# Idle matmuls, partly in fp32, around value units 1 and 2 of a decode attention block

## The chip, the cores and the metric

The kernel runs on one core of one Trainium2 chip. The metric is device microseconds (us) of one execution, the median of several. A profiled execution also gives a span, from its first to its last instruction; in the runs here the time is 1.8 to 2.4 us more than the span, and that difference varies, so where a few tenths matter this text compares spans. Before the prediction there were three timed runs of the kernel, 669.61 to 669.99 us, and one profiled run, 672.52 us (span 670.3).

## The reference, cut to what matters

```python
# B=8 sequences, one new token each; 32 query heads, 8 key/value heads, 8192 cached positions, Dh=128
h = layernorm(x) * (1 + ca) + sa                  # adaLN: sa .. gb come from silu(c) @ w_mod
q = (h @ wq) ...
p = softmax(q @ k_cache^T * Dh**-0.5)             # k_cache, v_cache: (8, 8, 8192, 128) bf16
x = x + ga * ((p @ v_cache) @ wo)
h = layernorm(x) * (1 + cb) + sb
x = x + gb * (relu(h @ w1 + b1)**2 @ w2 + b2)     # 512 -> 1792 -> 512
```

The two caches are 268 MB of the 283.65 MB that the kernel reads. All else is small.

## The kernel before

Per batch there are four key units and four value units of 4 MB (two heads each), loaded into a ring of four slots in the order k0..k3, v0..v3. TensorE transposes the keys and makes the scores; after the softmax it multiplies each value unit. A slot is loaded again once its reader is done. After the last batch's last value unit (which comes in four pieces) the MLP weights W1 and W2 are loaded into a freed slot, W2 in four pieces, so they are the last bytes to arrive.

`pe_stream` is a helper for matmuls whose result nobody reads: they only keep TensorE busy.

```python
def pe_stream(n, at):                       # n matmuls IDENT x (IDENT four times): 128x128 by 128x512, bf16
    rhs = IDENT[:, :].unsqueeze(1).to_broadcast([128, 4, 128])
    ts = [op("tensor", lambda e: e.matmul(
        bank(at).rearrange("p (a r) -> p a r", a=4), IDENT[:, :], rhs)) for _ in range(n)]
    return ts[0]
...
# softmax of a batch
t = op("vector", ... Dm ...)
pe_stream(5, 4)
t = op("tensor", lambda e: e.matmul(T_ps, R4[:], Dm[:]), [t, stg_free[3]])
... negm ...
pe_stream(5, 4)
... exps, transposes of P ...
# the value units of a batch, p = 0..3
for p in range(NP):
    ...
    for m in range(32):                     # value matmuls, wait for the load
        t = op("tensor", ... Obank[32*cg:32*(cg+1), :] ..., [loaded[n], k_rinv] + pmd[m // 8])
    t = op("vector", lambda e: e.tensor_copy(osb, Obank), [t])
    for i in range(4):                      # matmuls with SEL, wait for the copy
        t = op("tensor", ... oT_ps, osb[...], SEL[:, i, :] ..., [k_osb, k_all])
        if i == 0:
            released[n % NSLOT] = t         # the slot's next load may start
            ...
    if p == NP - 3:                         # value unit 1
        pe_stream(5, 4)
    ... norm_last = op("vector", ... oTn ...)
    if lastb and p == NP - 2:               # only in the last batch, after unit 2:
        k_proj = project(permute(...))      # 24 projection matmuls for heads of units 0..2
... last batch only: unit 3 in pieces (16 matmuls, then 8 fp32 ones for the projection, then 12, then a rest),
    layer norm, first layer (56 matmuls), second layer (56 matmuls, each waits for its W2 piece), output
```

Of the kernel before, what the change touches and what calls it, by code (L numbers as in the profile page):

```python
# [33 lines left out]
class Prog:  # L34
# [19 lines left out]
    def op(self, eng, fn, deps=()):  # L54
        o = Op(eng, fn, deps, None, self.at)
        o.tok = Tok(o, self.at)
        self.ops[eng].append(o)
        return o.tok
# [110 lines left out]
def bass_adaLN_cond__gqa_block_cached__dense_activation_squared_relu__decode_kernel(  # L169
    nc, A_x, A_k_cache, A_v_cache, A_wq, A_wo, B_x, B_w1, B_b1, B_w2, B_b2, c, w_mod, out):  # L170
    B, _, D = A_x.shape
    _, HKV, SK, DH = A_k_cache.shape
# [6 lines left out]
    NP = HKV // 2  # L179
# [7 lines left out]
    with ExitStack() as es:  # L187
# [26 lines left out]
        ONES = sb("ONES", [128, 128], FP32)  # L214
# [51 lines left out]
        bank = lambda i: PS[:, i, :]  # L266
# [4 lines left out]
        op, dma = Pg.op, Pg.dma  # L271
# [189 lines left out]
        def pe_stream(n, at):  # L461
            rhs = IDENT[:, :].unsqueeze(1).to_broadcast([128, 4, 128])
            ts = [op("tensor", lambda e: e.matmul(  # L463
                bank(at).rearrange("p (a r) -> p a r", a=4), IDENT[:, :], rhs)) for _ in range(n)]
            return ts[0]

        def key_tiles(n, k, half):

            src = tiles(n % NSLOT)
            toks = []  # L470
            for j in range(4):
                for i in range(8):
                    t = op("tensor", lambda e, j=j, i=i: e.matmul(  # L473
                        STG[j][:, i, :], src[:, 32 * k + 8 * j + i, :], IDENT[:, :], is_transpose=True),
                        [loaded[n], stg_free[j]])
                dst = KTb[:, half, 8 * j:8 * (j + 1), :]
                if (4 * k + j) % 8 in (1, 4, 7):
                    stg_free[j] = op("scalar", lambda e, j=j, dst=dst: e.activation(dst, STG[j], ACT.Copy), [t])  # L478
                else:
                    stg_free[j] = op("vector", lambda e, j=j, dst=dst: e.tensor_copy(dst, STG[j]), [t])  # L480
                toks.append(stg_free[j])
            return t, toks
# [40 lines left out]
        for b in range(B):  # L523
# [5 lines left out]
            for p in range(NP):  # L529
                n = 2 * NP * b + p  # L530
                for k in range(4):
                    t, toks = key_tiles(n, k, qn % 2)
                    if pend is not None:
                        maxes.append(scores(b, *pend))
                    if k == 3:
                        released[n % NSLOT] = score_first[0]
                        load(n + NSLOT)
                    pend = (p, k, qn % 2, toks)
                    qn += 1
# [3 lines left out]

            t = op("vector", lambda e: e.tensor_reduce(m1[:], m4[:], AX.X, ALU.max), maxes)
            t = op("vector", lambda e: e.tensor_scalar(Dm[:], Qmask[:], m1[:, 0:1], None, ALU.mult), [t, k_all])
            pe_stream(5, 4)
            T_ps = bank(7)[:, 0:4]
            t = op("tensor", lambda e: e.matmul(T_ps, R4[:], Dm[:]), [t, stg_free[3]])
            t = op("vector", lambda e: e.tensor_reduce(mq[:], T_ps, AX.X, ALU.max), [t])
            k_neg = op("vector", lambda e: e.tensor_scalar(negm[:], mq[:], -inv_sqrt, None, ALU.mult), [t])  # L550
            pe_stream(5, 4)
            exps = []
            for k in range(4):
                exps.append(op("scalar", lambda e, k=k: e.activation(  # L554
# [43 lines left out]
            for p in range(NP):  # L598
                if p == NP - 1:
                    Pg.at = "post" if lastb else (b, "b")  # L600
                n = 2 * NP * b + NP + p
# [3 lines left out]
                if not lastu:  # L605
                    for m in range(32):
# [4 lines left out]
                            tile_position=(0, 32 * cg)),  # L611
                            [loaded[n], k_rinv] + pmd[m // 8])
                    osb = O_sb[:, p % 2, :]
                    t = op("vector", lambda e, osb=osb, Obank=Obank: e.tensor_copy(osb, Obank), [t])  # L614
                    oT_ps = Obank[:, 0:8]
                    k_osb = t
# [6 lines left out]
                            if n + NSLOT < len(units):  # L623
                                load(n + NSLOT)
                    if p == NP - 3:
                        pe_stream(5, 4)
                    s_bank_free[p] = norm_last = op("vector", lambda e, p=p, b=b, oT_ps=oT_ps: e.tensor_tensor(  # L627
                        oTn_p[:, :, p, :, Pg.index(b)].rearrange("p h r o -> p h (r o)"), oT_ps.rearrange("p (h r) -> p h r", h=2), rinv_p[:, :, p, :], ALU.mult),
                        [t])
# [157 lines left out]
```

## Time and profile before

| | before |
|---|---|
| timed runs | 669.61, 669.77, 669.99 us |
| profiled run | 672.52 us, span 670.3 us, mean granted clock 0.894 |
| read from HBM | 283.66 MB |

Three lines of the page's slices (40 equal slices of 16.8 us; digits are tenths; PEclk is the granted TensorE clock):

```profile
PEclk9997996799969998799978998599977999699985
DMA  9999999999999999999999999999999999999994
GB/s 374 436 409 432 434 430 428 430 432 436 432 428 430 432 436 432 428 430 434 434 434 428 428 434 434 434 430 426 434 434 434 430 428 432 434 434 430 428 413 196
```

The DMA engines are busy throughout at 426 to 436 GB/s, except at the start and in the last two slices. The body of the kernel is bound by the transfers.

The timeline of TensorE (start us, duration us, line, operation, number of instructions, in brackets the idle time before and what ended it), first around the value units of batch 6, then the end, in the last batch:

```profile
563.67 1.24 PE L463 MATMUL PS<-IDENT 128*128 128x512 bf16 x5
566.41 1.91 PE L608 MATMUL PS<-ring,Pm 128*32 128x512 bf16 x32 [1.50 <-DMA ring<-in_A_v_cache_dram]
...
576.12 3.48 PE L608 MATMUL PS<-ring,Pm 128*32 128x512 bf16 x32 [6.75 <-DMA ring<-in_A_v_cache_dram]
...
585.84 5.51 PE L473 MATMUL PS<-IDENT,ring 128*128 128x128 bf16 x64 [5.17 <-DMA ring<-in_A_k_cache_dram]
...
641.76 1.24 PE L463 MATMUL PS<-IDENT 128*128 128x512 bf16 x5
644.12 3.58 PE L608 MATMUL PS<-ring,Pm 128*32 128x512 bf16 x32 [1.12 <-DMA ring<-in_A_v_cache_dram]
...
649.97 1.76 PE L517 MATMUL PS<-wo_sb,KTb 128*32 128x512 bf16 x24 [0.51 <-DVE KTb L512]
...
651.86 1.90 PE L662 MATMUL PS<-ring,Pm 128*32 128x512 bf16 x16
...
654.23 1.88 PE L673 MATMUL PS<-SELP,KTb 128*128 128x8 f32 x8
656.03 1.47 PE L662 MATMUL PS<-ring,Pm 128*32 128x512 bf16 x12
...
665.68 1.65 PE L737 MATMUL PS<-KTb,ring 128*128 128x8 bf16 x56 [0.97 <-DVE KTb L733]
```

Batches 0 to 6 have long waits for the next load behind units 1 and 2 and before the next key unit: a slower or faster TensorE changes nothing there. The last batch's unit 2 (at 644.12) takes 3.58 us for work that took 1.91 us in batch 6. After it TensorE hardly waits for a load again; the second layer (at 665.68) waited for VectorE, not for its weights.

The windows of the end (each line: window, its length, busy time of PE, PEld, DVE, ACT, POOL with the number of instructions, then granted clock, DMA share, GB/s):

```profile
640.80:644.20 3.40, 1.48 (x17) 0.58 (x17) 0.88 (x2) 0.00 (x0) 0.00 (x0) 1.00 0.91 390
644.20:647.60 3.40, 3.40 (x32) 1.03 (x32) 0.00 (x0) 0.00 (x0) 0.00 (x0) 0.50 0.99 419
647.60:651.00 3.40, 1.71 (x44) 0.92 (x44) 1.24 (x3) 0.00 (x0) 0.00 (x0) 1.00 0.98 402
651.00:654.40 3.40, 3.40 (x47) 1.33 (x36) 0.69 (x1) 0.00 (x0) 0.00 (x0) 0.50 1.04 411
654.40:668.00 13.60, 10.17 (x214) 7.93 (x214) 3.78 (x17) 0.27 (x1) 0.00 (x0) 0.50 0.55 217
```

In this run the changes of the clock lie on a grid: from the fall at 572.52 to the one at 644.20 there are 21 steps of 3.413 us. On this grid each window's clock answers to how full the one before it was: after 1.48 busy us of 3.40 the clock is halved, after a full window it is restored, after 1.71 us it is halved again. The window from 651.0 is full by its bars and the clock is not restored; it holds many matmuls of 8 columns, so the bars seem not to measure exactly what the clock follows. Below, work at half clock is called cold and work at full clock warm; the phase of a run is where its grid of clock windows lies.

### The profile page before, as it was taken

The page shows a single profiled execution, that of the slowest core. Times are in us where ns is not written, and L with a number is a line of the kernel's source. Part 1 is how long each engine was busy: PE and PEld are TensorE (multiplying, and loading weights), DVE is VectorE, ACT ScalarE, POOL GpSimd, SP SyncE. Part 2 cuts the span into 40 slices and gives each one's busy share as a digit, 9 for nine tenths or more (in the row PEclk, how much of TensorE's full clock was granted, in tenths as well). Part 3 has the DMA queues.
Part 4 walks back from the last instruction along what each step waited for, and adds up shares of the span by engine and source line. Part 5 has one row for each costly group of instructions (what it writes and reads, how often), then busy time and mean ns, then how long its engine had stood idle before and what let it go on. Part 6 is the DMA issues. An engine that isn't in the chain of part 4 may idle for free.

```text
span 670.3 us, 15469 instructions
## 1 busy us (share of the span) xinstructions
PE 498.0 (74%) x7056; PEld 340.4 (51%) x7056; DVE 302.5 (45%) x571; ACT 258.7 (39%) x289; POOL 18.4 (3%) x76
## 2 busy tenths in 40 slices
PE   3594963898549974699729985599746996299876
PEld 2384731775237741576308752377415763187425
DVE  1262731566216751467215661167414663066622
ACT  2152640466106650265405660166503662056600
POOL 7300000000000000000000000000000000000000
PEclk9997996799969998799978998599977999699985
DMA  9999999999999999999999999999999999999994
GB/s 374 436 409 432 434 430 428 430 432 436 432 428 430 432 436 432 428 430 434 434 434 428 428 434 434 434 430 426 434 434 434 430 428 432 434 434 430 428 413 196
DMA packets 12176, 283.85 MB, mean 423 GB/s; under 512 B 1250, under 2 KB 1283, under 8 KB 3588
## 3 DMA queue, kind: packets, MB, share of 16 engines
q1 hardware_dynamic: 12116, 283.65, 98.7%
q8 instruction: 9, 0.15, 0.1%
q10 hardware_dynamic: 48, 0.02, 0.0%
q14 instruction: 3, 0.02, 0.0%
HBM read 283.66 MB, written 0.01 MB: 423 GB/s over the span
## 4 chain that ended last, share of the span: by engine, by line
PE 51%; DMA 38%; ACT 6%; DVE 4%; issue 1%; SPq 0%; DVEq 0%
PE PS L473 35%; DMA ring<-in_A_k_cache_dram 32%; PE PS L490 9%; ACT P_sb L554 5%; DMA ring<-in_A_v_cache_dram 4%; PE PS L608 3%; DMA ring<-in_A_wq_dram 2%; ACT KTb L478 1%; DVE O_sb L614 1%; DVE m L497 1%; PE PS L566 1%; PE PS L662 0%; PE PS L463 0%; DVE Pm L580 0%; PE PS L586 0%
## 5 line engine op out<-in xcount | busy, mean ns | idle before, releaser
L478 ACT ACTIVATE KTb<-PS 128x1024 bf16<-128x1024 bf16 x192 | 196.5, 1024 | 331.1 <-PE PS L473 331.1
L473 PE MATMUL PS<-IDENT,ring 128*128 128x128 bf16 x4096 | 267.7, 228 | 49.6 <-DMA ring<-in_A_k_cache_dram 49.6
L473 PEld LDWEIGHTS PS<-IDENT,ring 128*128 128x128 bf16 x4096 | 247.1, 102 | 97.9 <-DMA ring<-in_A_k_cache_dram 50.8
L480 DVE COPY KTb<-PS 128x1024 bf16<-128x1024 bf16 x320 | 210.0, 687 | 143.0 <-PE PS L473 140.9
L608 PE MATMUL PS<-ring,Pm 128*32 128x512 bf16 x992 | 72.2, 442 | 55.2 <-DMA ring<-in_A_v_cache_dram 54.2
L490 PE MATMUL PS<-KTb,Qb 128*32 128x512 bf16 x1024 | 78.8, 384 | 4.5 <-ACT KTb L478 4.5
L614 DVE CAST O_sb<-PS 128x512 bf16<-128x512 f32 x31 | 21.4, 691 | 129.7 <-PE PS L608 129.7
L608 PEld LDWEIGHTS PS<-ring,Pm 128*32 128x32 bf16 x992 | 27.2, 107 | 90.8 <-DMA ring<-in_A_v_cache_dram 58.9
L554 ACT ACTIVATE P_sb<-PS,negm 128x1024 bf16<-128x1024 f32 x32 | 35.2, 1112 | 20.2 <-DVE negm L550 20.2
L463 PE MATMUL PS<-IDENT 128*128 128x512 bf16 x160 | 41.1, 379 | 0.0
L566 PE MATMUL PS<-IDENT,P_sb 128*128 128x128 bf16 x256 | 19.8, 220 | 16.1 <-ACT P_sb L554 16.1
L580 DVE COPY Pm<-PS 64x512 bf16<-64x512 bf16 x48 | 20.2, 421 | 25.0 <-PE PS L566 24.5
L618 PEld LDWEIGHTS PS<-SEL,O_sb 128*128 128x128 bf16 x124 | 5.2, 97 | 42.8 <-DVE O_sb L614 42.8
L566 PEld LDWEIGHTS PS<-IDENT,P_sb 128*128 128x128 bf16 x256 | 14.4, 98 | 24.1 <-ACT P_sb L554 24.1
L618 PE MATMUL PS<-SEL,O_sb 128*128 128x8 bf16 x124 | 7.9, 170 | 24.8 <-DVE O_sb L614 24.8
L490 PEld LDWEIGHTS PS<-KTb,Qb 128*32 128x32 bf16 x1024 | 15.4, 94 | 21.0 <-ACT KTb L478 8.5
L497 DVE TENSOR_REDUCE m<-PS 128x1 f32<-128x512 f32 x32 | 22.0, 689 | 6.6 <-PE PS L490 6.6
L463 PEld LDWEIGHTS PS<-IDENT 128*128 128x128 bf16 x160 | 13.5, 101 | 12.9 <-issue 3.4
L627 DVE TENSOR_TENSOR oTn<-PS,rinv 128x8 f32 x31 | 6.0, 194 | 14.2 <-PE PS L618 14.2
L478 ACT ACT_TABLE_LOAD x8 | 10.3, 1283 | 3.2 <-issue 3.2
L720 ACT ACTIVATE std<-PS,epst 128x8 f32<-128x8 f32 x1 | 0.3, 267 | 27.9 <-PE PS L719 27.9
L562 ACT ACTIVATE Pm<-PS 64x512 bf16<-64x512 bf16 x16 | 9.5, 592 | 2.7 <-PE PS L566 2.6
(130 smaller groups left out, 111.8 us busy)
## 6 DMA issues: line engine op xcount, KB each, us to landing
ring<-in_A_k_cache_dram SPq DMA_DIRECT2D x32, 4096.0 KB, 34.2
ring<-in_A_v_cache_dram SPq DMA_DIRECT2D x31, 4096.0 KB, 27.9
ring<-in_A_wq_dram SPq DMA_DIRECT2D x1, 4096.0 KB, 20.0
wo_sb<-in_A_wo_dram SPq DMA_DIRECT2D x1, 4096.0 KB, 47.6
ring<-in_w_mod_dram SPq DMA_DIRECT2D x1, 3072.0 KB, 10.5
ring<-in_A_v_cache_dram SPq DMA_DIRECT2D x1, 2048.0 KB, 23.1
ring<-in_B_w_dram SPq DMA_DIRECT2D x3, 512.0 KB, 19.9
ring<-in_B_w_dram SPq DMA_DIRECT2D x1, 1344.0 KB, 18.4
```

The lines of the kernel that those rows point to most:

```text
L463: ts = [op("tensor", lambda e: e.matmul(bank(at).rearrange("p (a r) -> p a r", a=4), IDENT[:, :], rhs)) for _ in range(n)]
L473: t = op("tensor", lambda e, j=j, i=i: e.matmul(STG[j][:, i, :], src[:, 32 * k + 8 * j + i, :], IDENT[:, :], is_transpose=True), [loaded[n ...
L478: stg_free[j] = op("scalar", lambda e, j=j, dst=dst: e.activation(dst, STG[j], ACT.Copy), [t])
L480: stg_free[j] = op("vector", lambda e, j=j, dst=dst: e.tensor_copy(dst, STG[j]), [t])
L490: t = op("tensor", lambda e, hf=hf, q=q, rhs=rhs: e.matmul(PS[32 * q:32 * (q + 1), k, :], Qb[:, 2 * p + hf, :], rhs, start=(p == 0 and hf ...
L497: return op("vector", lambda e: e.tensor_reduce(m4[:, k:k + 1], bank(k), AX.X, ALU.max), [t])
L554: exps.append(op("scalar", lambda e, k=k: e.activation(P_sb[:, k, :, :, :], bank(k).rearrange("p (i x) -> p i x", i=8).unsqueeze(2).to_bro ...
L566: t = op("tensor", lambda e, k=k, i=i: e.matmul(STG[k][:, i, :], P_sb[:, k, i, :, :].rearrange("p h x -> p (h x)"), IDENT[:, :], is_transp ...
L580: done.append(op("vector", lambda e, dst=dst, frm=frm: e.tensor_copy(dst, frm), [t, k_pm]))
L608: t = op("tensor", lambda e, p=p, m=m, cg=cg, vt=vt, Obank=Obank: e.matmul(Obank[32 * cg:32 * (cg + 1), :], lhs[:, p, 32 * m:32 * m + 32], ...
L614: t = op("vector", lambda e, osb=osb, Obank=Obank: e.tensor_copy(osb, Obank), [t])
L618: t = op("tensor", lambda e, i=i, osb=osb, oT_ps=oT_ps: e.matmul(oT_ps, osb[:, i * 128:(i + 1) * 128], SEL[:, i, :], start=(i == 0), stop= ...
```

## The change

Its intent is to fill TensorE's waits around value units 1 and 2 of every batch, so that the clock does not drop, and to use fp32 for part of it, where one matmul fills more TensorE time.

```diff
+        def pe_stream32(n, at):
+            rhs = ONES[:, :].unsqueeze(1).to_broadcast([128, 4, 128])
+            ts = [op("tensor", lambda e: e.matmul(
+                bank(at).rearrange("p (a r) -> p a r", a=4), ONES[:, :], rhs)) for _ in range(n)]
+            return ts[0]
@@ softmax, at two places
-            pe_stream(5, 4)
+            pe_stream32(1, 4)
+            pe_stream(1, 4)
@@ value unit, after its matmuls, before the matmuls with SEL
                     osb = O_sb[:, p % 2, :]
+                    if p == NP - 3:
+                        pe_stream32(1, 4)
+                    elif p == NP - 2:
+                        pe_stream(3, 4)
@@ value unit, after the matmuls with SEL
                     if p == NP - 3:
-                        pe_stream(5, 4)
+                        pe_stream32(2, 4)
+                    elif p == NP - 2:
+                        pe_stream(1, 4)
```

More of the change, by code (lines that the diff above doesn't have):

```diff
@@ L613, in bass_adaLN_cond__gqa_block_cached__dense_activation_squared_relu__decode_kernel @@
                     osb = O_sb[:, p % 2, :]
+                    if p == NP - 3:
+                        pe_stream32(1, 4)
+                    elif p == NP - 2:
+                        pe_stream(3, 4)
                     t = op("vector", lambda e, osb=osb, Obank=Obank: e.tensor_copy(osb, Obank), [t])
@@ L625, in bass_adaLN_cond__gqa_block_cached__dense_activation_squared_relu__decode_kernel @@
                     if p == NP - 3:
-                        pe_stream(5, 4)
+                        pe_stream32(2, 4)
+                    elif p == NP - 2:
+                        pe_stream(1, 4)
                     s_bank_free[p] = norm_last = op("vector", lambda e, p=p, b=b, oT_ps=oT_ps: e.tensor_tensor(
```

## The prediction

> **What bounds the kernel now.** The slices of the page show the DMA engines at 9 tenths in 39 of 40 slices, 426 to 436 GB/s from the fourth slice to the thirty-eighth; 283.65 MB come in. In the timeline every batch repeats after about 77.8 us, which is its eight 4 MB loads at that rate. In the chain of waits TensorE has 51%, but in each batch it waits again for data: in batch 6 (timeline) 1.50 us before value unit 2, 6.75 us before unit 3, 5.17 us before the next batch's first key unit. Loads are issued about 28 to 34 us before they land, so a release that slips by a microsecond starves nothing. Batches 0 to 6 are therefore DMA-bound, and what TensorE does in those waits is free and worth nothing.
>
> Only the end is bound by TensorE and its dependents: the last batch's value unit 2 lands at 644.12 and the kernel ends at 670.3. Those 26.2 us have hardly a DMA wait. The granted clock (windows of 0.5 us) is 1.0 until about 644.2, 0.5 until 647.8, 1.0 until 651.2, then 0.5 to the end. Value unit 2 takes 3.58 us there, 1.91 us at full clock (batch 6).
>
> **Why it drops.** The Trainium skill, "TensorE: Matmul & The Clock Gate", Part 1, says the clock is decided in free-running windows of 3.4 us by how busy the array was. The trace agrees: changes lie on a grid of 3.41 us (572.5, 579.3, 582.8, 589.5, 644.2). In the window 640.8 to 644.2 the array did little more than the five idle matmuls (1.24 us).[...]
>
> **What the change does, per batch.** At the softmax, 5 bf16 matmuls become one fp32 and one bf16, twice. At unit 1: one fp32 while VectorE copies (copy 0.69 us, gap 0.80 us), and two fp32 after in place of five bf16. At unit 2: three bf16 in the copy's gap, one after. A bf16 one costs about 0.216 us warm (five in 1.24). The fp32 ones with 32 columns appear as two instructions, 0.41 us a pair; estimating four passes of a bf16 stream plus exposed weight loads, one costs 0.9 to 1.25 us. So the softmax changes by 0 to +0.3 us, unit 1 gets 1.5 to 2.7 us more work, in a wait of 1.12 us plus the copy gap of 0.80 us.
>
> **Worth.** The window to 644.2 becomes 75 to 90% full: unit 2 runs warm, minus 1.67 us. The matmuls in its copy gap keep the next window full too, so the 24 projection matmuls and the 16 of the last unit (1.76 and 1.90 us, half or all cold) also run warm: up to minus 1.2 us, and the 8 fp32 plus 12 value matmuls perhaps minus 1.3. The tiny matmuls after that stay cold. Against it, an fp32 overrun may delay unit 2 by up to 0.7 us. And the last MLP weight piece lands near 663.3 us, against a second layer running 665.7 to 667.3: gains over about 3.8 us turn into a DMA wait.
>
> Sum: about minus 2.9 us, **666.9 us, range 665.3 to 669.0**. Faster by over 2%: 0.01; within 2%: 0.98; slower: 0.01.
>
> **What would show it.** DMA slices and the batch period unchanged; unit 2 of the last batch 1.9 us instead of 3.58, starting no later than 644.8; granted clock 1.0 from 644 to at least 651; mean clock slightly up from 0.894; last-unit matmuls 1.0 us instead of 1.9.
>
> **What would make it wrong.** fp32 matmuls not counting as activity, or running slower than four passes and delaying unit 2; the clock falling again one window later; the window grid lying elsewhere in unprofiled runs.

## The result, and the profile after

| | before | changed |
|---|---|---|
| timed runs of the same rounds | 669.49 to 669.99, median 669.69 us (4) | 669.32 to 669.56, median 669.41 us (4) |
| ratio | | 0.9996, 95% interval 0.9978 to 1.0013: the same |
| profiled run | 672.52 us, span 670.3 | 669.43 us, span 667.6 |
| mean granted clock of the profiled run | 0.894 | 0.897 |

Here and below, a ratio is the mean time of one kernel's fast runs over that of the other's of the same rounds, so it is not quite the ratio of the medians quoted.

The two profiles differ by 2.7 us of span, nearly what was predicted. The times differ by 0.3 us. The same three slices of the changed kernel's page:

```profile
PEclk9696997899969998699977999699987999779996
DMA  9999999999999999999999999999999999999996
GB/s 376 431 412 437 426 427 435 432 430 430 434 434 430 430 432 436 428 432 432 436 428 430 434 434 430 430 434 434 428 432 434 434 426 434 432 434 428 434 415 264
```

The body is as DMA-bound as before. The end of the changed kernel's TensorE timeline:

```profile
641.50 1.12 PE L469 MATMUL PS<-ONES 128*128 128x512 f32 x2
642.46 0.24 PE L630 MATMUL PS<-SEL,O_sb 128*128 128x8 bf16 x4
642.56 1.96 PE L469 MATMUL PS<-ONES 128*128 128x512 f32 x4
644.46 1.91 PE L616 MATMUL PS<-ring,Pm 128*32 128x512 bf16 x32
...
648.64 1.48 PE L523 MATMUL PS<-wo_sb,KTb 128*32 128x512 bf16 x24 [0.51 <-DVE KTb L518]
...
650.23 1.05 PE L676 MATMUL PS<-ring,Pm 128*32 128x512 bf16 x16
...
651.74 1.06 PE L687 MATMUL PS<-SELP,KTb 128*128 128x8 f32 x8
652.73 0.83 PE L676 MATMUL PS<-ring,Pm 128*32 128x512 bf16 x12
...
661.68 1.02 PE L751 MATMUL PS<-KTb,ring 128*128 128x8 bf16 x32 [0.98 <-DVE KTb L747]
663.57 1.01 PE L751 MATMUL PS<-KTb,ring 128*128 128x8 bf16 x24 [0.87 <-DMA ring<-in_B_w_dram]
```

and the same stretches of time:

```profile
640.80:644.20 3.40, 3.40 (x26) 1.31 (x18) 0.88 (x2) 0.00 (x0) 0.00 (x0) 1.00 0.92 395
644.20:647.60 3.40, 3.35 (x41) 1.16 (x40) 0.72 (x2) 0.00 (x0) 0.00 (x0) 1.00 0.97 414
647.60:651.00 3.40, 2.73 (x61) 1.25 (x60) 1.21 (x3) 0.00 (x0) 0.00 (x0) 1.00 0.98 406
651.00:654.40 3.40, 2.60 (x43) 1.74 (x36) 0.69 (x1) 0.00 (x0) 0.00 (x0) 1.00 1.02 401
654.40:668.00 13.60, 7.29 (x194) 6.08 (x194) 3.51 (x17) 0.64 (x2) 0.00 (x0) 0.55 0.56 221
```

The stretch before unit 2 is now full, unit 2 takes 1.91 us, the projection and the last unit run at full clock, as forecast. But these stretches are windows of the first profile's grid, not of this run's. Here the clock falls only at 655.71, so that the edges lie, in steps of 3.413 us, at 638.65, 642.06, 645.47 and so on. Unit 2 began under the clock that the window from 638.65 set, with 2.61 busy us; the same stretch of the kernel before (0.34 us earlier, as unit 2 is) holds 2.17 us, more than the 1.50 and 1.72 after which its clock fell. By this estimate unit 2 would have been warm here without the change too. So this pair of profiles mixes the change with another phase; a pair at equal phase comes with e3 and e4. TensorE then reaches the second layer before its weights: the last line of the timeline waits 0.87 us for W2. The open question was why the timed runs show nothing of this. Two answers were in play. Either the profiled run of before was a rare, slow one and its typical runs have no cold tail to repair; or the timed runs of the changed kernel lose the gain again somewhere. That profiling itself slows a run is ruled out by the later profiles: several are of runs at 669.3 to 669.5 us (e2, e9, e10, e11).

### The profile page after: what moved, and what is told of

The parts are those of the page before. It is cut to its first block, busy times and chain, and to the rows that moved or that the text cites. A ratio compares the mean times of both kernels' runs of the same rounds, so it can differ in the third digit from the quotient of the medians.

```text
span 667.6 us, 15485 instructions
## 1 busy us (share of the span) xinstructions
PE 513.8 (77%) x7064; PEld 344.8 (52%) x7064; DVE 302.6 (45%) x571; ACT 258.7 (39%) x289; POOL 18.4 (3%) x76
## 4 chain that ended last, share of the span: by engine, by line
PE 52%; DMA 37%; ACT 7%; DVE 2%; SPq 1%; issue 1%
PE PS L479 36%; DMA ring<-in_A_k_cache_dram 32%; PE PS L496 9%; ACT P_sb L562 5%; PE PS L616 2%; DMA ring<-in_B_w_dram 2%; DMA ring<-in_A_wq_dram 2%; PE PS L469 1%; SPq L659 1%; ACT KTb L484 1%; DVE O_sb L626 1%; PE PS L463 1%; PE PS L574 1%; DVE Pm L588 0%; PE PS L594 0%
## 5 line engine op out<-in xcount | busy, mean ns | idle before, releaser
L616 PE MATMUL PS<-ring,Pm 128*32 128x512 bf16 x992 | 70.4, 434 | 46.8 <-DMA ring<-in_A_v_cache_dram 45.9
L469 PE MATMUL PS<-ONES 128*128 128x512 f32 x80 | 42.1, 630 | 0.0
L463 PE MATMUL PS<-IDENT 128*128 128x512 bf16 x88 | 26.9, 380 | 0.0
L469 PEld LDWEIGHTS PS<-ONES 128*128 128x128 f32 x80 | 12.7, 190 | 10.6 <-issue 10.6
L463 PEld LDWEIGHTS PS<-IDENT 128*128 128x128 bf16 x88 | 7.7, 105 | 9.1 <-issue 7.2
```

Source lines behind the costliest of these rows:

```text
L463: ts = [op("tensor", lambda e: e.matmul(bank(at).rearrange("p (a r) -> p a r", a=4), IDENT[:, :], rhs)) for _ in range(n)]
L469: ts = [op("tensor", lambda e: e.matmul(bank(at).rearrange("p (a r) -> p a r", a=4), ONES[:, :], rhs)) for _ in range(n)]
L616: t = op("tensor", lambda e, p=p, m=m, cg=cg, vt=vt, Obank=Obank: e.matmul(Obank[32 * cg:32 * (cg + 1), :], lhs[:, p, 32 * m:32 * m + 32], ...
```

## The experiments

Twelve kernels ran. In e1 to e4, e5 to e8, and e9 with e10, the kernels of one group shared a chip and nine runs of before. In the expectation of e5 the count of earlier runs should read 13 of 19, and in that of e9 nine spans above 668.3, not ten.

### e1: the kernel before, again

No edit.

> The kernel before, unchanged, so that a second profile of it and more of its times exist. The only profile of before is of a run of 672.52 us, 2.8 us above its own timed median (669.69). Theory (clock phase): that run was the rare one, in which the 3.41 us clock windows fell so that value unit 2 of the last batch ran at half clock; a typical run has it at full clock (about 1.9 us, not 3.6) and ends about 3.4 us after the last MLP weight piece lands, span 667.5 to 668.2, time 669.4 to 670.0; about one run in ten is near 672.5. Rival (given back): typical runs of before have the cold unit 2 too, the profile is as representative as any, and the new profile shows unit 2 at about 3.6 us with a span near 670.

Measured: 669.28, 669.60, 670.65, 670.76, 670.97 us; before in the same rounds 669.31 to 670.66 (nine runs, two of them at 670.65 and above). The median, 670.65, is outside the expected range, and slow runs are far more frequent than one in ten. What the profile shows is closer to the rival's forecast: a cold unit 2. The profile fell on the run of 670.97 us (span 669.1). Lines of its timeline:

```profile
644.33 3.54 PE L608 MATMUL PS<-ring,Pm 128*32 128x512 bf16 x32 [1.18 <-DMA ring<-in_A_v_cache_dram]
...
650.14 1.88 PE L517 MATMUL PS<-wo_sb,KTb 128*32 128x512 bf16 x24 [0.51 <-DVE KTb L512]
...
652.14 1.90 PE L662 MATMUL PS<-ring,Pm 128*32 128x512 bf16 x16
...
655.51 0.83 PE L662 MATMUL PS<-ring,Pm 128*32 128x512 bf16 x12
```

Unit 2 and the first part of the last unit are cold, the later part is not. So the same kernel's times come in levels: near 669.5, near 670.8, and once 672.5. The three timed runs before the prediction all lay in the lowest.

### e2: before without the idle matmuls after unit 1

```diff
-                    if p == NP - 3:
-                        pe_stream(5, 4)
```

> Before without the five idle matmuls after value unit 1. Theory (clock phase): the nearly empty stretch from the end of unit 1 to unit 2 of the last batch is then about 3.3 us, one clock window long, so that unit 2 runs at half clock in most runs (an estimate: three of four), and those end 2 to 3 us later: median 671.5 to 672.8, with some runs near 669.7. Rival (idle matmuls in this wait never matter, the end is set by the weight load alone): every run 669.4 to 670.0.

Measured: 669.26, 669.48, 670.88, 670.92, 671.01 us (spans 667.4, 667.6, 669.0, 669.1, 669.2). Three of five are slow; they are about 1.6 us above the other two, not 2 to 3. The profile fell on the fastest run, and shows why the size was wrong:

```profile
644.30 3.21 PE L608 MATMUL PS<-ring,Pm 128*32 128x512 bf16 x32 [2.04 <-DMA ring<-in_A_v_cache_dram]
...
649.77 1.48 PE L517 MATMUL PS<-wo_sb,KTb 128*32 128x512 bf16 x24 [0.51 <-DVE KTb L512]
...
651.36 1.05 PE L660 MATMUL PS<-ring,Pm 128*32 128x512 bf16 x16
```

Unit 2 is mostly cold (3.21 us) and the span is 667.4 all the same, as short as any of before. One cold group cost nothing here; something else sets the end. The slow runs do not show that the five idle matmuls matter: the unedited kernel, in e1, had three slow runs of five as well.

### e3 and e4: both kernels without the last two weight pieces

A wrong result; TensorE's work is the same.

```diff
-  ... for i, (a, z, j) in enumerate(((0, 4, 4), (4, 8, 4), (8, 12, 4), (12, 14, 2)))]
+  ... for i, (a, z, j) in enumerate(((0, 4, 4), (4, 8, 4)))]
-      yT_ps[:, k, :], W2v[:, f, ...], hidT[:, f, :], ... [k_sq[f // 7], d_w2[f // 4]])
+      yT_ps[:, k, :], W2v[:, f % 8, ...], hidT[:, f, :], ... [k_sq[f // 7], d_w2[f % 8 // 4]])
```

> Before, wrong result on purpose: the last two MLP weight pieces (768 KB) are not loaded, the second layer reads the first eight tiles again, the TensorE work is the same. It takes the weight load off the end. Theory (the end of a typical run of before is already close to the weight-load floor): the time falls by 0 to 1 us against before in typical runs, to 668.7 to 669.7, as TensorE's chain then sets the end. Rival (before is set by TensorE's chain well above the floor): no change at all, 669.6 to 669.9.

> The changed kernel with the same pieces not loaded, wrong result on purpose. Its profile showed 0.87 us of waiting for the weight piece in the second layer, and its runs are all at 669.3 to 669.6. Theory (floor): without the floor it gains about 1 us, to 668.1 to 668.8, and is then faster than e3 by 0 to 1.5 us. Rival (the change gives its gain back on TensorE, for example by the fp32 matmuls overrunning the wait): it stays at 669.3 to 669.6, and is not faster than e3.

Measured for before without them (e3): 668.28, 668.42, 669.74, 669.93, 670.03 us. The changed kernel without them (e4): 668.14 to 668.48 us, all five (mean 668.32 against 669.28 of e3). The range for e4 held; the one for e3 missed, because e3 has two levels 1.5 us apart rather than one.

This is the clearest pair. With the weight load out of the way the changed kernel falls from 669.41 to 668.31 us (medians of different rounds; the changed kernel's in e9 was 669.57), and before's slow level stands apart from its fast one by 1.5 us. So the fast level of both kernels at 669.3 to 670.0 is set by the landing of W2 (the floor, in these texts), about 1.1 us later than TensorE's warm chain alone would end. The changed kernel gives nothing back on TensorE.

The profile of e4 is also the one that shows the change at work on the clock. Its clock falls at 654.48, so a window starts at 640.82, within 0.04 us of those of the slow profiles of before (640.78 in the first, 640.85 in e1). There it holds 3.13 busy us instead of 1.50 and 1.49, and the next one 3.15; the clock stays whole, and unit 2 takes 1.91 us instead of 3.58 and 3.54:

```profile
640.82:644.24 3.42, 3.13 (x14) 1.15 (x10) 0.88 (x2) 0.00 (x0) 0.00 (x0) 1.00 0.85 364
```

### e5 and e6: the two parts of the change alone

e5 has only the fp32 matmuls around unit 1, e6 only the bf16 ones around unit 2.

```diff
 e5: osb = O_sb[:, p % 2, :]          e6: osb = O_sb[:, p % 2, :]
+    if p == NP - 3:                 +    if p == NP - 2:
+        pe_stream32(1, 4)           +        pe_stream(3, 4)
 ...                                  ...
     if p == NP - 3:                      if p == NP - 3:
-        pe_stream(5, 4)                      pe_stream(5, 4)
+        pe_stream32(2, 4)           +    elif p == NP - 2:
                                     +        pe_stream(1, 4)
```

> Before with only the change's part around value unit 1 (one fp32 matmul in the copy's gap, two after it). Runs of before so far: 12 of 18 unprofiled-or-profiled timings at 669.3 to 670.0, 5 at 670.6 to 671.0, one at 672.5. Theory (clock phase under a weight-load floor): filling the wait keeps unit 2 of the last batch at full clock in every run, so all five times lie at 669.2 to 670.0 and unit 2 takes 1.9 us in the profile. Rival (the slow runs have another cause): one or two of five runs stay above 670.5, as in before.

> Before with only the change's part around value unit 2 (three bf16 matmuls in the copy's gap, one after). Theory: it comes too late for unit 2 itself, which still takes 3.2 to 3.6 us in about a third of the runs, but it keeps the next window full, so that the projection and the last unit run at full clock; a cold unit 2 costs 1.7 us, of which the floor hides about 1.3: all times 669.2 to 670.2. Rival (only unit 1's wait decides): a third of the runs at 670.6 to 671.0 as before.

Measured: e5 669.49 to 670.10 us (spans 667.6 to 668.3), unit 2 at 1.91 us in its profile; e6 669.52 to 670.50 us (spans 667.7 to 668.2). The nine runs of before beside them: 669.24 to 671.16 us, spans 667.4 to 669.3, three of them 668.7 and above. Both upper ends of time were missed, by 0.1 and 0.3 us, on a chip whose times lay up to 2.4 us above the spans; by span both parts kept the end at 668.3 or below. In the profile of e6 unit 2 still takes 3.46 us, as expected, and the groups behind it are warm:

```profile
644.75 3.46 PE L614 MATMUL PS<-ring,Pm 128*32 128x512 bf16 x32 [1.27 <-DMA ring<-in_A_v_cache_dram]
648.14 0.82 PE L463 MATMUL PS<-IDENT 128*128 128x512 bf16 x3
...
650.48 1.48 PE L523 MATMUL PS<-wo_sb,KTb 128*32 128x512 bf16 x24 [0.51 <-DVE KTb L518]
```

These two profiles have nearly the same phase. The window from 641.04 in e5 holds 3.18 busy us, the one from 641.10 in e6 1.59 us, and only the second is followed by half clock: the fp32 matmuls count as activity. In its one profile e5 has no cold group from unit 2 to the last unit, and e6 has one; the other runs of each have no trace, but no span above 668.3.

### e7 and e8: the changed kernel with TensorE delayed on purpose

One or three more fp32 idle matmuls after unit 2.

```diff
                     elif p == NP - 2:
                         pe_stream(1, 4)
+                        pe_stream32(1, 4)      # e8: pe_stream32(3, 4)
```

> The changed kernel with one more fp32 idle matmul (0.96 us each in the changed kernel's trace) after value unit 2, in front of the last batch's projection: a pure delay of TensorE's chain at full clock. Theory (floor: the changed kernel ends 1.3 us later than its TensorE chain alone would, 667.6 against 666.3 us of span in e4): no change against the changed kernel, 669.2 to 669.7. Rival (TensorE's chain sets the end): 670.2 to 670.5.

> The same with three more, 2.9 us of delay. Theory: 2.9 minus the 1.3 us of slack, so 1.3 to 1.8 us above the changed kernel, 670.7 to 671.3. Rival (TensorE's chain sets the end): 672.1 to 672.5. Second rival (the end does not depend on TensorE at all): 669.2 to 669.7.

Measured: e7 669.38 to 670.18 us, spans 667.5 to 667.9; its step after unit 2 starts at 648.47 instead of 647.82, so that the delay was 0.65 us, not 0.96. e8 670.50 to 671.02 us, spans 668.2 to 669.2. By span, e7 is the changed kernel (667.5 to 667.7 at first); its times missed their range by the same varying offset as e5's. The rival, with every delay visible, would have put e8 near 670.0 in span; its median of 670.55 us lies 0.15 us below the expected range. In e8's profile the step after unit 2 starts at 650.17 instead of 647.82, so the delay was 2.35 us, not 2.9: the rest fell into a wait that was there already.

```profile
647.50 2.74 PE L469 MATMUL PS<-ONES 128*128 128x512 f32 x6
650.17 0.31 PE L514 MATMUL PS<-oTn,PERM 128*32 128x48 bf16 x16
...
664.02 1.65 PE L752 MATMUL PS<-KTb,ring 128*128 128x8 bf16 x56 [0.98 <-DVE KTb L748]
```

The second layer no longer waits for W2. The slack of the changed kernel's profile: its second layer starts at 661.68 and, as in the profile of e4, would let the output transposes start 1.94 us later, at 663.62; they started at 664.87. That is 1.25 us, and 2.35 minus 1.25 is 1.1 us: the span of e8's profile is 668.7, against 667.6.

### e9 and e10: the changed kernel again, and a bf16 version of its first part

e10 fills unit 1's waits with `pe_stream(4, 4)` and `pe_stream(8, 4)` in place of the fp32 matmuls, with nothing else changed from before.

> The changed kernel again, on a fresh chip beside before. So far its four spans are 667.5 to 667.7, while before's 24 spans with a record run from 667.4 to 670.3 and ten of them are above 668.3. Theory: the change only removes the slow phases; all its spans are 667.3 to 668.2, the fastest run of before is as fast as its fastest (within 0.3 us), and its mean is 0.3 to 0.9 us below before's. Rival (the change shifts all runs, or none): its spans spread to 669 as before's do, or its fastest run beats before's fastest by over 0.5 us.

> Before with bf16 idle matmuls of about the same TensorE time around unit 1 (four in the copy's gap, eight after it) in place of the fp32 ones. Theory (only the filling of the wait counts): unit 2 takes 1.9 us, spans 667.3 to 668.3 like the kernel with only the fp32 part. Rival (fp32 matmuls keep the clock up in a way that bf16 ones do not): some spans above 668.5 and a unit 2 of over 3 us in them.

Measured: e9 669.45 to 670.05 us, spans 667.6 to 668.2; e10 669.28 to 669.84 us, spans 667.4 to 668.0, unit 2 at 1.91 us. The spans lie as expected. But before, in the nine runs beside them, had no slow run either (spans 667.4 to 668.3, times 669.24 to 670.38), so the expected advantage of the mean did not appear: 669.73 for e9, 669.69 for before. The profile of e10 does not tell bf16 from fp32: unit 2 began under the clock of a window (638.29 to 641.70) that had 2.61 busy us, mostly of value unit 1. Behind it the window filled mostly by the bf16 matmuls, 3.23 us, kept its clock, as the one filled with fp32 did in e5. No slow run of e10 or of before was there to compare.

### e11 and e12: two more looks at before

No edit.

> One more profile of the kernel before, unchanged: both profiles of it so far are of slow runs (spans 670.3 and 669.1, unit 2 of the last batch 3.58 and 3.54 us). Theory: if this run's span is below 668.2, its tail shows full clock through the projection and the last unit (the 24 projection matmuls 1.5 us and the 16 of the last unit 1.05 us), whether or not unit 2 itself was cold, and its second layer waits for the last weight piece or starts within 1 us of it. If the span is above 668.5, unit 2 takes over 3 us and one of those two groups is cold as well. Rival (slow and fast runs differ elsewhere): a fast run with the same cold tail, or a slow run with a warm one.

> The same once more, with the same expectation for each state of the run.

Measured: 669.49 us (span 667.7) and 669.88 us (span 668.0), one run each, both of the fast level. e11 is the typical run that was missing:

```profile
641.47 1.24 PE L463 MATMUL PS<-IDENT 128*128 128x512 bf16 x5
644.12 1.91 PE L608 MATMUL PS<-ring,Pm 128*32 128x512 bf16 x32 [1.42 <-DMA ring<-in_A_v_cache_dram]
...
648.30 1.48 PE L517 MATMUL PS<-wo_sb,KTb 128*32 128x512 bf16 x24 [0.51 <-DVE KTb L512]
...
649.89 1.05 PE L662 MATMUL PS<-ring,Pm 128*32 128x512 bf16 x16
...
661.41 1.01 PE L737 MATMUL PS<-KTb,ring 128*128 128x8 bf16 x32 [0.97 <-DVE KTb L733]
663.64 1.02 PE L737 MATMUL PS<-KTb,ring 128*128 128x8 bf16 x24 [1.22 <-DMA ring<-in_B_w_dram]
```

The five idle matmuls and an idle wait (1.42 us, 1.12 in the slow profile) stand in front of unit 2, and it is warm all the same. The phase differs: this run's window starts 0.61 us earlier, takes in more of value unit 1, and holds 1.73 busy us where the slow profile's held 1.50:

```profile
640.17:643.58 3.41, 1.73 (x17) 0.50 (x9) 0.89 (x2) 0.00 (x0) 0.00 (x0) 1.00 0.91 389
```

Its tail is that of the changed kernel, with the same wait for W2. In e12 unit 2 is warm (1.91 us) but the projection and the 16 matmuls of the last unit are not (2.23 and 1.83 us): a fast run with a partly cold tail, which my expectation had excluded. Of the 1.95 us by which its chain is later than e11's, all but about 0.4 us is hidden (spans 668.0 and 667.7).

## Why the prediction was wrong

The tails of the six profiles of before and of the changed kernel, in us:

| run | unit 2 starts | unit 2 | projection x24 | last unit x16 | fp32 x8 | last unit x12 | wait for W2 | span |
|---|---|---|---|---|---|---|---|---|
| before, first profile | 644.12 | 3.58 | 1.76 | 1.90 | 1.88 | 1.47 | none | 670.3 |
| before, e1 | 644.33 | 3.54 | 1.88 | 1.90 | 1.06 | 0.83 | none | 669.1 |
| before, e12 | 644.54 | 1.91 | 2.23 | 1.83 | 1.06 | 0.83 | none | 668.0 |
| before, e11 | 644.12 | 1.91 | 1.48 | 1.05 | 1.06 | 0.83 | 1.22 | 667.7 |
| changed, first profile | 644.46 | 1.91 | 1.48 | 1.05 | 1.06 | 0.83 | 0.87 | 667.6 |
| changed, e9 | 644.38 | 1.91 | 1.48 | 1.05 | 1.06 | 0.83 | 0.98 | 667.6 |

The five groups sum to 10.59, 9.21, 7.86 and 6.33 us in the four runs of before. In e11 the output transposes start at 664.94, and without waits they would start 1.94 us after the second layer, at 663.35: a slack of 1.59 us. Adding to e11's span the extra TensorE time and the later start of unit 2, less that slack, gives 670.4, 669.2 and 668.1 for the other three, against 670.3, 669.1 and 668.0 measured. So the end is the later of two things, the landing of W2 and TensorE's chain, and in these four runs of before the level is explained by how many groups of that chain run at half clock, with the start of unit 2.

Point by point:

- **"Batches 0 to 6 are DMA-bound ... worth nothing": right.** The slices are unchanged and e7 and e8, which put more idle work into every batch, cost only at the end.
- **"The window to 644.2 becomes 75 to 90% full: unit 2 runs warm, minus 1.67 us": right in the trace.** 3.58 became 1.91 us, and the next groups became warm too. In that pair of profiles it was partly luck of the phase; at equal phase e4 shows it (3.13 busy us against 1.50). The fp32 size was right as well: 0.96 us from the start of one to the next instruction, inside 0.9 to 1.25.
- **"Gains over about 3.8 us turn into a DMA wait": the floor is there, but it lies nearer.** It was placed from the slow profile by when W2 would land. There the last piece landed 13.7 us after it was issued; in the changed kernel's profile it took 14.7 us and was issued 0.2 us later, so the landing was mis-sized by about 1.2 us (why it takes 13.7 us in some runs and up to 15.0 in others stays open). The second layer started 4.0 us earlier, and 1.25 us of that was lost in the wait; 2.7 us of span were left.
- **"Sum: about minus 2.9 us, 666.9 us": the step that failed.** The sum was costed in the trace of a run of 672.52 us and then subtracted from the timed median of 669.77 us. Those are different states of the same kernel, and the saving counts only in the one that it was costed in: the profiled run had nearly the whole tail cold, while runs at the timed level, as e11 and e12 show, have it warm or cold in a part that the floor hides. Subtracted from its own run, 672.52 minus 2.9 is 669.6 us; the changed kernel measured 669.41. That this sum fits so well is partly luck: the second layer started 4.0 us earlier, and a nearer floor took 1.25 us of it. The evidence stood in the table: a profiled run 2.8 us above three timed runs that agree within 0.4 us is not a picture of them. The floor also forbids 666.9 us: with W2 loaded no run here had a span below 667.4, which is a time of about 669.2 us.
- **The last doubt, "the window grid lying elsewhere in unprofiled runs", is the one that the later profiles bear out:** in e11, at the timed level, the window's edge lies at 640.17 instead of 640.78, and in e12 at 639.06 and 642.47. Runs without a kept trace show no grid. The doubt had been given no weight in the number or the range.

The Trainium skill, "TensorE: Matmul & The Clock Gate", Part 1, had the warning: the window is free-running and "run-variable", so the same kernel gets different cold counts according to where the window lies at kernel start. The profiles agree: with five idle matmuls and a wait of 1.12 to 1.42 us in front, unit 2 took 3.58, 3.54 and 1.91 us in three profiles of one kernel, whose windows started at 640.78, 640.85 and 640.17.

What the change is good for: of the 36 recorded spans of before, nine lie above 668.3 us; of the nine of the changed kernel, none does, nor of the fifteen of e5, e7 and e10, which fill unit 1's wait as well (nor of the five of e6, which does not). Most of that difference rests on single chips: on the chip of e5 to e8 it was three of nine against none of ten (e5 and e7), on the chip of e9 none of nine against none of five. That the change keeps the tail warm in the phase that made before slow is shown by e4's profile, and e3 against e4 (three slow of five, none of five) agrees; that it does so in every phase is not shown. Its worth in a mean over many chips is at most a few tenths of a microsecond and was not measured apart from noise. Why slow runs were frequent in one set of rounds and absent in another stays open; the share of phases was not controlled. No version with a right result beats both kernels by more than the noise.

## What to carry to other kernels

Before costing anything from a trace, compare the profiled run's own time with the timed runs; if it stands apart by as much as the effect you are after, the trace shows another state, and the saving must be subtracted from that run, not from the median. A stage whose clock depends on the phase, as unit 2 here with 1.91 to 3.58 us, has a spread of outcomes, not one duration, so look at two or three profiles of it, and lay the windows on each run's own grid. And when a chain's end has a second bound close by, here the last weight piece, work out that end first: it says how much any saving can be worth.

## What the Trainium skill lacked or had wrong

- "TensorE: Matmul & The Clock Gate", Part 1, gives no filling at which a warm clock is lost. Here, on each run's own grid of 3.41 us windows, those around unit 2 with 1.49 to 1.72 us of busy bars were followed by half clock (before, e1, e6, e12), and those with 1.73 us (e11), 1.80 us (e10) and more were not. In the later stages, with many matmuls of 8 columns, the clock was lost after fuller windows too (2.81 us in e11).
- The same page, Part 4, says that the full clock does not engage for transpose-mode matmuls. Here it does: batch 7's first key unit starts at 585.84 us in the first profile of before with nothing but such transposes, 64 of them in 5.51 us, and 32 of the same take 1.96 us at full clock afterwards (from 591.83).
- The same page, Part 1, puts the penalty of the clock's ramp under 1% of a span for modelling. That holds (667.4 to 670.3 us, 0.4%), but it was ten times the difference between the two kernels' medians (0.3 us), and no page says to check a profiled run against the timed ones.
- "FP8 and Floating Point Precision", TensorE Precision Notes, gives four passes for true fp32. The runs agree: an fp32 128x512 matmul took 0.96 us against 0.22 us for a bf16 one, shown as two instructions. No page says whether fp32 counts as activity for the clock; it did (e5: a window of 3.18 us, mostly fp32, kept the clock, where e6 with 1.59 us at the same phase lost it).
